# Attention backward, last units of the core: dK on two sets of 32x32 array tiles and dQ transposed in halves

## Chip, cores, metric

The kernel runs on one core of a Trainium2 chip. The metric is the device time of one execution in microseconds (us), smaller is better.

## What is computed

The reference concatenates two attention blocks over 2048 tokens of width 448 and returns the output and all gradients. The part that the change touches is the backward pass of block B (16 heads of width Dh = 28, one shared K and V head):

```python
def _B_ref(x, wq, wk, wv, wo):
    q = (x @ wq).reshape(B, S, H, Dh).transpose(0, 2, 1, 3)
    k, v = x @ wk, x @ wv
    p = softmax(einsum("bhqd,bkd->bhqk", q, k) * Dh ** -0.5)
    o = einsum("bhqk,bkd->bhqd", p, v)
    return o.transpose(0, 2, 1, 3).reshape(B, S, H * Dh) @ wo
_out, _vjp = jax.vjp(_f, ...)       # both blocks
_grads = _vjp(grad_out)
```

Out of it come dQ, dK and dV, and from these the gradients of the input (`out_4`, here dx), of wq (`out_5`), wk, wv (`out_6`, `out_7`) and wo (`out_8`).

## The kernel before

Block A and the projections of block B come first and fill some 215 us. The rest is one software pipeline, written out by hand under `manual_schedule` (in it every engine and queue keeps the order of the program): a loop over `u` from 0 to 539. A *unit* is 256 keys by two heads by 256 queries; a *block* `b` (of 64) is 8 units. Unit `u` computes scores for `u` (while `u < 512`), the product with dO for `w = u - 16`, its dS (VectorE L936 for one head; ScalarE L938 and GpSimd L939 for the other), the sums for o and dQ, the transposed dS for `y = u - 18`, and on odd `u` four of a block's 16 steps of dK (`dk_m`, L839). From `u = 512` on no scores are left: these last 28 units are the drain.

- **dK.** One step `dk_m` is four matmuls of 32 rows by 32 columns by 512 moving columns, on the diagonal tiles (32a, 32a) of the array; all add into one PSUM bank, `dk_acc`. In the drain the odd units 519 to 537 do it.
- **dQ** of block `b` is copied into `qT_B[g]` (L955), the last block at `u = 531`. At `u = 531` four DMA transposes of 128x2048 (L995, SyncE queue, one for each `g`) make `dqn`, dQ by tokens, which the gradient of wq needs.
- **Loads for the tail** (`post_load`, every even `u` from 512 to 528, SyncE queue): four loads of the output gradient (L757), four of x (L762), at `u = 528` the transposed weights `wqT` (L752). Behind that last one 14 small GpSimd DMAs (L754) put four rows each of the transposed wk and wv into unused rows of `wqT`. They overwrite what the load has brought, so they wait for it.
- **Gradient of wo** (`gwo`, from `u = 520`): 64 matmuls in PSUM banks SB[0] and SB[1]; each of four results is copied by ScalarE (L775) and stored by four GpSimd DMAs (L778, 16 in all). The last two output tiles of block B (`out_proj`, `u = 532` and 536) use SB[2] and are stored by GpSimd (L729).
- **The tail**, after the loop, is ordered by the scheduler, which may also pull its instructions up between those of the loop. VectorE copies dV out of PSUM (L1021, four), VectorE and ScalarE copy dK in turn (L1026, L1028, two each), both into `dkvT`. Then 14 small DMAs, the *pads* (L1067, seven on SyncE, seven on GpSimd in turn), put rows of `dkvT` into unused rows of `qT_B`, so that one product with `wqT` gives all of dx. TensorE does `dwq(0)`, `dwq(1)` (gradient of wq, from `dqn`) with the transposes of `dkvT`, `dx(0)` to `dx(4)`, `dwq(2)`, `dwq(3)`, the gradients of wk and wv, and `dx(5)` to `dx(15)`. The PSUM banks rotate: `dwq(2)` writes the bank of `dx(0)`.

```python
for n, (g, r, c) in enumerate(PADS):     # g = n // 4; c: row of dkvT, dK for n < 7, dV from n = 7 on
    [nc.sync, nc.gpsimd][n % 2].dma_start(qT_B[g].rearrange("(j r) s -> j r s", r=32)[:, r, :], dkvT[c:c + 4, :])
```

Of the kernel before, what the change touches and what calls it, by code (L numbers as in the profile page):

```python
# [8 lines left out]
ACT = mybir.ActivationFunctionType  # L9
ALU = mybir.AluOpType  # L10
AX = mybir.AxisListType
BF16 = mybir.dt.bfloat16
F32 = mybir.dt.float32

H = 16
DH = 28
D = 448
P = 128
# [7 lines left out]
def kernel(  # L26
# [21 lines left out]
    nc = tc.nc  # L48
# [3 lines left out]
    scale = float(DH) ** -0.5  # L52
# [35 lines left out]
    def flat(t):  # L88
        return t.rearrange("p a b -> p (a b)")
# [537 lines left out]
    NB = 64  # L627
    NU = NB * 8
    qT_B = [R1[:, g, :] for g in range(4)]
    vaug, kn, do_nat = vaug_, kn_, R2x[:, 0:NS, :]  # L630
    with ExitStack() as cs_:
        pe_ = cs_.enter_context(tc.tile_pool(name="ceT", bufs=1, side="right"))
        pn_ = cs_.enter_context(tc.tile_pool(name="ceN", bufs=1, side="right"))
        pd_ = cs_.enter_context(tc.tile_pool(name="cdsT", bufs=5, side="right"))
        pqa_ = cs_.enter_context(tc.tile_pool(name="cqXa", bufs=1, side="right"))
        px_ = cs_.enter_context(tc.tile_pool(name="cdsx", bufs=2, side="right"))
# [4 lines left out]
        SB = [psA.tile([P, 512], F32, name="aacc") for i in range(3)]  # L641
        DB = [psA.tile([P, 512], F32, name="agen") for i in range(2)]
        oq, dk_acc = (psA.tile([P, 512], F32, name="agen") for _ in range(2))

        dsT, dsx, qX, don, doT, rl, prod = ({} for _ in range(7))
        ETs = [pe_.tile([P, 4, 2, 512], BF16, name=f"eT{i}") for i in range(5)]
        ENs = [pn_.tile([P, 32, P], BF16, name=f"eN{i}") for i in range(6)]
# [7 lines left out]
        def mmt(out, lhsT, rhs, pos, start, stop):  # L655
            nc.tensor.matmul(out, lhsT=lhsT, rhs=rhs, start=start, stop=stop, tile_position=pos,  # L656
                             skip_group_check=True)

        def blk(b):
            qc, pair = divmod(b, 8)  # L660
            return qc, pair, pair // 2, pair % 2

        def rows_SD(u, sp, dp):
            b, tp = divmod(u, 8)
            w = u - 16
            qc, pair, g, hp = blk(b)
            todo = [(0, 0), (0, 1), (1, 0), (1, 1)] * 2
            if sp is not None and dp is not None and u % 2 == 0:
                todo = [(0, 0), (0, 1), (1, 0)] * 2 + [(1, 1)] * 2
            seen = {}  # L670
            for d in todo:
                if (dp if d[0] else sp) is None:
                    continue
                k, h = d
                t2 = seen.get(d, 0)
                seen[d] = 1
                t = 2 * tp + t2
                tc_ = slice(t * P, (t + 1) * P)
                oc = slice(t2 * 256, (t2 + 1) * 256)
                r = 64 * (1 - hp if k else hp) + 32 * h  # L680
                if k:
                    mmt(dp[h][:, oc], vT_rep[r:r + 32, tc_], doT[w // 8][r:r + 32, :], (r, 0), True, True)
                else:
                    mmt(sp[h][:, oc], kT_rep[r:r + 32, tc_], qT_B[g][r:r + 32, qc * 256:(qc + 1) * 256],
                        (r, 0), True, True)
# [45 lines left out]
        def by_tokens(t):  # L731
            return t.rearrange("p (t d) -> p t d", d=512)

        post = {"gb": [], "xb": []}
# [30 lines left out]
        def gwo(n0, n1):  # L765
            for n in range(n0, n1):
# [6 lines left out]
                if st == NS - 1:  # L773
                    sb = pd_.tile([P, 2, 512], BF16, name="dsT")[:, 0, 0:D]
                    nc.scalar.activation(out=sb, in_=al[:, 0:D], func=ACT.Copy)  # L775
                    for j in range(4):
                        h = 4 * g_ + j
                        nc.gpsimd.dma_start(out_8[h * DH:(h + 1) * DH, :], sb[32 * j + 1:32 * j + 1 + DH, :])  # L778

        GW = [0, 0, 4, 4, 10, 10, 16, 16, 22, 22, 28, 28, 34, 34, 40, 40, 48, 48, 56, 56, 64, 64]  # L780
        onps, tps2 = {}, {}

# [53 lines left out]
            nc.sync.dma_start_transpose(qX[qc].rearrange("p b s c -> p (b s) c")[:, :, g * P:(g + 1) * P],  # L836
                                        st.rearrange("p n a j -> p (n a j)"))

        def dk_m(b, m):  # L839
            qc, pair, g, hp = blk(b)  # L840
            h, B, s = m // 8, (m // 2) % 4, m % 2
            for a in range(4):
                rhs = dsx[b][32 * a:32 * a + 32, :, h, :, :].rearrange(
                    "p u t (b i s) -> p u t b i s", b=4, s=2)[:, :, :, B, :, s]
                mmt(dk_acc[32 * a:32 * a + 32, :],
                    qX[qc][32 * a:32 * a + 32, B, s, pair * 64 + 32 * h:pair * 64 + 32 * h + 32],
                    rhs, (32 * a, 32 * a), b == 0 and m == 0, b == NB - 1 and m == 15)

        def o_mm(v):
            b, tp = divmod(v, 8)  # L850
# [16 lines left out]
        def o_dq(vs, ys):  # L867
            for v, y in zip(vs, ys):
                todo = [f(i) for f, i in ((o_mm, v), (dq_mm, y)) if 0 <= i < NU]
                for _ in range(2):  # L870
                    for g_ in todo:
                        next(g_)

        def dv_mm(dv_acc, b, h, qb):
            for c in range(4):
                rhs = eN(b, c).rearrange("p (u h t q) k -> p u h t q k", u=2, h=2,
                                                       t=2)[:, :, h, :, qb, :]
                mmt(dv_acc[32 * c:32 * c + 32, :], don[b][:, qb, h, :], rhs, (0, 32 * c),
                    b == 0 and h + qb == 0, b == NB - 1 and h + qb == 2)
# [15 lines left out]
        with tc.manual_schedule():  # L895
            nc.sync.dma_start(wo, wo_d[:, 0:D].rearrange("(g p) c -> p g c", p=P))
            qX[0] = pqa_.tile([P, 4, 2, 512], BF16, name="qX")
            for g in range(4):
                st = pd_.tile([P, 2, 512], BF16, name="dsT").rearrange("p a (n j) -> p a n j", j=32).rearrange(
                    "p a (n b) j -> p (a n) b j", b=4)  # L900
# [3 lines left out]
            for u in range(NU + 28):  # L904
                w = u - 16
                hasS = u < NU
                hasD = 0 <= w < NU
                sp = [SB[(2 * u + h) % 3] for h in range(2)] if hasS else None
                dp = DB if hasD else None
                spare = SB[(2 * u + 2) % 3] if hasS else SB[2]  # L910
                rows_SD(u, sp, dp)
                if (b := due(u, 10)) is not None:
                    onat_T(b, spare)
# [11 lines left out]
                if u == 1:  # L925
                    q_shift(pn3, shifts[3], [pd_.tile([P, 2, 512], BF16, name="dsT").rearrange("p a b -> p (a b)").bitcast(F32)
                                             for _ in range(1)])
                    dv_acc = psA.tile([P, 512], F32, name="aacc")
# [24 lines left out]
                if (b := due(u, 27)) is not None:  # L953
                    qc, pair, g, hp = blk(b)
                    nc.vector.tensor_scalar(out=qT_B[g][64 * hp:64 * hp + 64, qc * 256:(qc + 1) * 256],  # L955
                                            in0=oq[64:128, 0:256], scalar1=scale, scalar2=None, op0=ALU.mult)
# [20 lines left out]
                if u % 2:  # L977
                    b, i = divmod(u - 27, 8)
                    if 0 <= b < NB:
                        for m in range(2 * i, 2 * i + 4):  # L980
                            dk_m(b, m)
                else:
                    o_dq((u - 2, u - 1), (u - 20, u - 19))
                    b, n = divmod(u - 20, 8)
                    for k in {0: (0, 1), 2: (2,), 6: (3,)}.get(n, ()) if 0 <= b < NB else ():
                        dv_mm(dv_acc, b, k // 2, k % 2)
                y = u - 18

                if 512 <= u < 530 and u % 2 == 0:
                    post_load((u - 512) // 2)  # L990
                if u == 531:
                    dqn = px_.tile([P, 8, 2, 2, 256], BF16, name="dsx").rearrange("p a b c d -> p (a b c d)").rearrange(
                        "p (t d) -> p t d", d=512)
                    for g_ in range(4):
                        nc.sync.dma_start_transpose(dqn[:, :, g_ * P:(g_ + 1) * P], qT_B[g_])  # L995
                if u >= 519:
                    gwo(GW[u - 519], GW[u - 518])

                if 0 <= y < NU:
                    b, tp = divmod(y, 8)  # L1000
                    if tp == 0:
                        dsx[b] = px_.tile([P, 8, 2, 2, 256], BF16, name="dsx")
                    nc.vector.transpose(  # L1003
                        out=dsx[b][:, tp, :, :, :].rearrange("p h t c -> p (h t c)").bitcast(F32),
                        in_=dsT[y][:, :, :].rearrange("p h c -> p (h c)").bitcast(F32))

        dkvT, wqT, xb = post["dkvT"], post["wqT"], post["xb"]
# [10 lines left out]
            return pd_.tile([P, 2, 512], BF16, name="dsT")[:, 0, :]  # L1018

        for c in range(4):  # L1020
            nc.vector.tensor_copy(out=dkvT[32:64, c * 512:(c + 1) * 512], in_=dv_acc[32 * c:32 * c + 32, :])  # L1021
        for c in range(4):
            t = dkvT[0:32, :].rearrange("p (t a i) -> p t a i", a=4, i=32)[:, :, c, :]
            src = dk_acc[32 * c:32 * c + 32, :].rearrange("p (t i) -> p t i", i=32)
            if c % 2:
                nc.vector.tensor_scalar(out=t, in0=src, scalar1=scale, scalar2=None, op0=ALU.mult)  # L1026
            else:
                nc.scalar.activation(out=t, in_=src, func=ACT.Copy, scale=scale)  # L1028

        def dwq(c):  # L1030
            r = DC_ROWS[c]
            al = gen(0)
            for st in range(NS):
                rhs = dqn[:, st, :].rearrange("p (h c) -> p h c", c=32)[:, :, 1:1 + DH]
                if c == 3:
                    half_mm(al, xb[st][:, 3 * P:D], rhs, st)
                else:
                    mm(al[:, 0:D], xb[st][:, c * P:(c + 1) * P], rhs, start=(st == 0), stop=(st == NS - 1))
            sb = sbuf()[:, 0:D]
            if c == 3:  # L1040
                odd = pd_.tile([P, 2, 512], BF16, name="dsT").rearrange("p a b -> p (a b)").bitcast(F32)[0:64, 0:D]
                nc.scalar.activation(out=odd, in_=al[64:128, 0:D], func=ACT.Copy)
                nc.vector.tensor_tensor(out=sb[0:64], in0=al[0:64, 0:D], in1=odd, op=ALU.add)
            else:
                nc.vector.tensor_copy(out=sb[0:r], in_=al[0:r, 0:D])
            nc.sync.dma_start(out_5[c * P:c * P + r, :], sb[0:r])
# [27 lines left out]
        for c in range(2, 4):  # L1074
            dwq(c)
        for c in range(4):
            r = DC_ROWS[c]
            ps = gen(0)
            for st in range(NS):
# [3 lines left out]
                                 func=ACT.Copy)  # L1083
# [35 lines left out]
```

## Time and profile before

| | |
|---|---|
| median of 3 runs | 1066.45 us (1065.12 to 1068.38) |
| span of the profiled execution | 1064.7 us |
| TensorE busy over the span | 1023.1 us (96%) |
| VectorE, ScalarE, GpSimd busy | 899.5 (84%), 870.4 (82%), 780.7 us (73%) |
| 16 DMA engines, hardware queue of SyncE | 99.6% of the span |
| dK steps of the drain begin | 1000.65 us (`u` = 519) ... 1030.11 us (`u` = 537) |
| `dwq(0)`, `dx(0)`, `dwq(2)` begin on TensorE | 1033.27, 1040.65, 1044.87 us |
| last matmul begins, span ends | 1060.39 (four of them), 1064.7 us |

Times inside the profile are us from the start of the span. The profiled execution's span of 1064.7 us is 1.75 us below the median of the timed runs. A line of the timeline gives start, length, engine, line of the kernel, operation, written and read tiles and count; behind it the idle time before it and what ended that. An entry of the GpSimd queue that is a DMA is the time in which GpSimd makes its descriptors; its data land later.

### The profile page before, as it was taken

The page shows a single profiled execution, that of the slowest core. Times are in us where ns is not written, and L with a number is a line of the kernel's source. Part 1 is how long each engine was busy: PE and PEld are TensorE (multiplying, and loading weights), DVE is VectorE, ACT ScalarE, POOL GpSimd, SP SyncE. Part 2 cuts the span into 40 slices and gives each one's busy share as a digit, 9 for nine tenths or more (in the row PEclk, how much of TensorE's full clock was granted, in tenths as well). Part 3 has the DMA queues.
Part 4 walks back from the last instruction along what each step waited for, and adds up shares of the span by engine and source line. Part 5 has one row for each costly group of instructions (what it writes and reads, how often), then busy time and mean ns, then how long its engine had stood idle before and what let it go on. Part 6 is the DMA issues. An engine that isn't in the chain of part 4 may idle for free.

```text
span 1064.7 us, 40036 instructions
## 1 busy us (share of the span) xinstructions
PE 1023.1 (96%) x16241; PEld 489.1 (46%) x16241; DVE 899.5 (84%) x1797; ACT 870.4 (82%) x1741; POOL 780.7 (73%) x1033
## 2 busy tenths in 40 slices
PE   9999999998999999999999999999999999999998
PEld 5555455434444444444444444444444444444444
DVE  7887400459999999999999999999999999999942
ACT  6463222489999999999999999999999999999522
POOL 6001242218888898899889989988998999888881
PEclk9999999999999999999999999999999999999999
DMA  9849899079999999999999999999999999999963
GB/s 264 167 108 192 171 203 246 22 137 181 193 188 196 182 203 189 188 202 191 197 181 197 181 196 195 193 189 194 196 197 192 199 190 183 208 190 177 222 141 89
DMA packets 689937, 195.15 MB, mean 183 GB/s; under 512 B 670616, under 2 KB 687792, under 8 KB 689752
## 3 DMA queue, kind: packets, MB, share of 16 engines
q1 hardware_dynamic: 680152, 179.92, 99.6%
q0 software_dynamic: 4640, 8.71, 2.9%
q10 hardware_dynamic: 4960, 3.96, 1.3%
q8 instruction: 127, 2.08, 0.8%
q14 instruction: 58, 0.48, 0.2%
HBM read 12.60 MB, written 10.84 MB: 22 GB/s over the span
## 4 chain that ended last, share of the span: by engine, by line
PE 43%; ACT 32%; issue 14%; POOL 5%; DVE 4%; DMA 1%; ACTq 0%; DVEq 0%; POOLq 0%
ACT cp L938 16%; PE agen L81 14%; ACT eT L970 13%; PE agen L656 10%; PE aacc L656 10%; PE aacc L81 5%; POOL dsT L939 3%; PE aacc L790 2%; ACT eT L924 2%; PE aacc L821 1%; DVE dsT L936 1%; DVE dsx L1003 1%; DMA out_dram<-dsT 1%; POOL eT L754 1%; POOL out_dram L778 0%
## 5 line engine op out<-in xcount | busy, mean ns | idle before, releaser
L939 POOL TENSOR_TENSOR dsT<-cp,eT 128x512 bf16<-128x512 bf16 x512 | 587.9, 1156 | 78.9 <-ACT cp L938 71.7
L1003 DVE STREAM_TRANSPOSE dsx<-dsT 128x512 f32<-128x512 f32 x512 | 357.6, 699 | 2.9 <-POOL dsT L939 0.8
L656 PEld LDWEIGHTS <-R 32*128 32x128 bf16 (+1 forms) x9104 | 227.9, 94 | 274.1 <-issue 238.4
L936 DVE TENSOR_TENSOR dsT<-agen,eT 128x512 bf16<-128x512 f32 x512 | 341.7, 667 | 10.9 <-PE agen L656 5.6
L938 ACT ACTIVATE cp<-agen 128x512 bf16<-128x512 f32 x512 | 315.8, 617 | 12.3 <-PE agen L656 11.2
L924 ACT ACTIVATE eT<-aacc 128x512 bf16<-128x512 f32 x512 | 313.6, 612 | 14.8 <-PE agen L656 4.8
L970 ACT ACTIVATE eT<-aacc 128x512 bf16<-128x512 f32 x512 | 322.2, 629 | 0.0
L656 PE MATMUL agen<-dsx,qX 32*32 32x512 bf16 x4096 | 267.6, 375 | 0.0
L656 PE MATMUL agen<-doT,R 32*128 32x256 bf16 x2048 | 247.1, 269 | 3.4 <-DVE dsT L936 1.4
L656 PE MATMUL aacc<-R,R 32*128 32x256 bf16 (+1 forms) x2240 | 218.2, 268 | 7.2 <-DVE oTs L800 2.5
L656 PE MATMUL agen<-eT,R 128*32 128x256 bf16 x2048 | 157.5, 274 | 0.1
L656 PE MATMUL agen<-dsT,R 128*32 128x256 bf16 x2048 | 156.8, 274 | 0.1
L656 PEld LDWEIGHTS <-qX 32*32 32x32 bf16 x4096 | 79.8, 89 | 113.7 <-issue 53.3
L656 PE MATMUL aacc<-eN,don 128*32 128x512 bf16 x1024 | 97.1, 379 | 0.1
L81 PEld LDWEIGHTS <-R 128*128 128x128 bf16 (+1 forms) x517 | 40.8, 98 | 43.5 <-issue 11.5
L406 POOL COPY pk<-R 128x256 bf16<-128x256 bf16 x4 | 1.6, 397 | 73.8 <-DVE R L366 73.7
L81 PE MATMUL agen<-R,R 128*128 128x448 bf16 (+1 forms) x180 | 42.1, 361 | 0.6 <-ACT R L225 0.6
L832 POOL COPY qst<-R 128x512 bf16<-128x512 bf16 x56 | 34.2, 611 | 4.0 <-DMA qX<-qst 3.9
L656 PEld LDWEIGHTS <-don 128*32 128x32 bf16 x1024 | 33.8, 97 | 1.4 <-issue 1.0
L804 POOL TENSOR_TENSOR prod<-R,oTs 128x128 f32<-128x128 bf16 x64 | 27.6, 431 | 9.3 <-DVE oTs L800 9.3
L422 DVE TENSOR_TENSOR osb<-aacc,pr 64x448 bf16<-64x448 f32 x2 | 1.2, 618 | 38.3 <-DMA out_dram<-osb 24.4
L955 DVE TENSOR_SCALAR R<-agen 64x256 bf16<-64x256 f32 x64 | 27.3, 427 | 3.6 <-PE agen L656 1.6
(231 smaller groups left out, 967.8 us busy)
## 6 DMA issues: line engine op xcount, KB each, us to landing
out_dram<-osb ACTq DMA_DIRECT2D x22, 112.0 KB
eN<-eT SPq DMA_TRANSPOSE x128
xa<-in_A_x_dram SPq DMA_DIRECT2D x8, 224.0 KB
ga<-in_grad_out_dram SPq DMA_DIRECT2D x4, 448.0 KB
xa<-in_grad_out_dram POOLq DMA_DIRECT2D x4, 448.0 KB, 6.1
out_dram<-wdq POOLq DMA_DIRECT2D x8, 224.0 KB, 4.0
eT<-in_grad_out_dram SPq DMA_DIRECT2D x4, 448.0 KB
eT<-in_B_x_dram SPq DMA_DIRECT2D x4, 448.0 KB
```

The lines of the kernel that those rows point to most:

```text
L81: nc.tensor.matmul(out_ap, lhsT=lhsT, rhs=rhs, start=start, stop=stop, tile_position=(0, 0))
L656: nc.tensor.matmul(out, lhsT=lhsT, rhs=rhs, start=start, stop=stop, tile_position=pos, skip_group_check=True)
L790: nc.tensor.transpose(onp[:, qb, :, :].rearrange("p h c -> p (h c)"), oTs[0:64, qb * P:(qb + 1) * P], identF[0:64, 0:64], tile_position=(0 ...
L804: nc.gpsimd.tensor_tensor(out=prod[b][:], in0=dnv, in1=os_, op=ALU.mult)
L832: eng.tensor_copy(out=st.rearrange("p (b s) a j -> p b s a j", s=2)[:, :, s, :, :], in_=src.unsqueeze(2).to_broadcast([P, 4, 4, 32]))
L924: nc.scalar.activation(out=eT(u)[:, 0, :], in_=sp[0][:, :], func=ACT.Exp, scale=scale)
L936: nc.vector.tensor_tensor(out=dst[:, 0, :], in0=dp[0][:, :], in1=ew[:, 0, :], op=ALU.mult)
L938: nc.scalar.activation(out=cp[:, :], in_=dp[1][:, :], func=ACT.Copy)
L939: nc.gpsimd.tensor_tensor(out=dst[:, 1, :], in0=cp[:, :], in1=ew[:, 1, :], op=ALU.mult)
L955: nc.vector.tensor_scalar(out=qT_B[g][64 * hp:64 * hp + 64, qc * 256:(qc + 1) * 256], in0=oq[64:128, 0:256], scalar1=scale, scalar2=None, ...
L970: nc.scalar.activation(out=eT(u)[:, 1, :], in_=sp[1][:, :], func=ACT.Exp, scale=scale)
L1003: nc.vector.transpose(out=dsx[b][:, tp, :, :, :].rearrange("p h t c -> p (h t c)").bitcast(F32), in_=dsT[y][:, :, :].rearrange("p h c -> p ...
```

## The change

Four edits, all in the drain and the first lines of the tail. In the odd units 519 to 535 every second dK step uses the tiles (32a, 32((a+2) mod 4)) and adds into a bank of its own, `dk_two` = SB[2]; unit 537 goes on as before. The last two output tiles move from SB[2] to DB[1] and DB[0]. dQ by tokens is no longer made at `u = 531` by four transposes of 128x2048, but by eight of 128x1024 into two freed buffers of transposed e: two at `u = 523`, two at 525, two at 527, one at 529, one at 531. dV is copied by ScalarE at `u = 533`, `dk_two` (scaled, with the rows put back) by ScalarE at `u = 536`, and VectorE adds the two halves of dK in four instructions in place of the four copies.

```diff
+        dqn = [by_tokens(flat(ENs[(124 + c) % 6])) for c in range(2)]
...
-        def dk_m(b, m):
+        dk_two = SB[2]
+
+        def dk_m(b, m, other=0):
...
-                mmt(dk_acc[32 * a:32 * a + 32, :],
+                k = 32 * ((a + 2) % 4) if other else 32 * a
+                mmt((dk_two if other else dk_acc)[k:k + 32, :],
                     qX[qc][32 * a:32 * a + 32, B, s, pair * 64 + 32 * h:pair * 64 + 32 * h + 32],
-                    rhs, (32 * a, 32 * a), b == 0 and m == 0, b == NB - 1 and m == 15)
+                    rhs, (32 * a, k), other == 2 or b == 0 and m == 0, other == 0 and b == NB - 1 and m == 15)
...
-                spare = SB[(2 * u + 2) % 3] if hasS else SB[2]
+                spare = SB[(2 * u + 2) % 3] if hasS else DB[u // 4 % 2] if u > 530 else SB[2]
...
-                            dk_m(b, m)
+                            dk_m(b, m, (1 + (u == 519 and m == 2 * i + 1)) * (m % 2) if 519 <= u < 537 else 0)
...
                 if 512 <= u < 530 and u % 2 == 0:
                     post_load((u - 512) // 2)
-                if u == 531:
-                    dqn = px_.tile([P, 8, 2, 2, 256], BF16, name="dsx").rearrange("p a b c d -> p (a b c d)").rearrange(
-                        "p (t d) -> p t d", d=512)
-                    for g_ in range(4):
-                        nc.sync.dma_start_transpose(dqn[:, :, g_ * P:(g_ + 1) * P], qT_B[g_])
+                for v, half, gs in ((523, 0, (0, 1)), (525, 0, (2, 3)), (527, 1, (0, 1)), (529, 1, (2,)), (531, 1, (3,))):
+                    for g_ in gs if u == v else ():
+                        nc.sync.dma_start_transpose(dqn[half][:, :, g_ * P:(g_ + 1) * P],
+                                                    qT_B[g_][:, half * 1024:half * 1024 + 1024])
+                if u == 533:
+                    for c in range(4):
+                        nc.scalar.activation(out=post["dkvT"][32:64, c * 512:(c + 1) * 512], in_=dv_acc[32 * c:32 * c + 32, :],
+                                             func=ACT.Copy)
+                if u == 536:
+                    dk_sum = pd_.tile([P, 2, 512], BF16, name="dsT").rearrange("p a b -> p (a b)").bitcast(F32)
+                    for c in range(2):
+                        r = 64 * (1 - c)
+                        nc.scalar.activation(out=dk_sum[64 * c:64 * c + 64, :], in_=dk_two[r:r + 64, :], func=ACT.Copy,
+                                             scale=scale)
...
-            nc.vector.tensor_copy(out=dkvT[32:64, c * 512:(c + 1) * 512], in_=dv_acc[32 * c:32 * c + 32, :])
-        for c in range(4):
...
-            if c % 2:
-                nc.vector.tensor_scalar(out=t, in0=src, scalar1=scale, scalar2=None, op0=ALU.mult)
-            else:
-                nc.scalar.activation(out=t, in_=src, func=ACT.Copy, scale=scale)
+            nc.vector.scalar_tensor_tensor(out=t, in0=src, scalar=scale,
+                                           in1=dk_sum[32 * c:32 * c + 32, :].rearrange("p (t i) -> p t i", i=32),
+                                           op0=ALU.mult, op1=ALU.add)
...
-                rhs = dqn[:, st, :].rearrange("p (h c) -> p h c", c=32)[:, :, 1:1 + DH]
+                rhs = dqn[st // 8][:, st % 8, :].rearrange("p (h c) -> p h c", c=32)[:, :, 1:1 + DH]
```

## Prediction

> **What bounds it now.** I read four views: TensorE's timeline of the drain, GpSimd's, SyncE's, and last the chain of waits. TensorE has no idle time from 1000.33 to 1020.28 and then only two gaps, 0.44 us before the second half of the gradient of wo and 0.50 us before `dwq(0)` (its 128x2048 transposes land late). So shorter dK steps do move TensorE forward. But GpSimd's timeline shows a second engine that never rests:
>
> ```profile
> 1012.10 2.45 POOL L939 TENSOR_TENSOR dsT<-cp,eT 128x512 bf16<-128x512 bf16 x2 [1.39 <-DVE dsT L936]
> 1015.72 1.16 POOL L939 TENSOR_TENSOR dsT<-cp,eT 128x512 bf16<-128x512 bf16 x1 [1.17 <-ACT cp L938]
> 1017.19 7.98 POOL L754 DMA_DIRECT2D eT<-wkvT_d  x14 [0.32 <-issue]
> 1025.17 4.06 POOL L778 DMA_DIRECT2D out_dram<-dsT  x8
> 1030.11 0.57 POOL L729 DMA_DIRECT2D out_dram<-R  x1 [0.88 <-DMA out_dram<-dsT]
> ...
> 1033.30 1.70 POOL L1067 DMA_DIRECT2D R<-eN  x3
> 1035.00 2.07 POOL L778 DMA_DIRECT2D out_dram<-dsT  x4
> 1037.06 2.25 POOL L1067 DMA_DIRECT2D R<-eN  x4
> ```
>
> 39 small DMAs run back to back from 1017.19 to 1039.31: 7.98 (14 x L754) + 8.13 (16 x L778) + 1.12 (2 x L729) + 3.95 (7 pads, L1067) = 21.2 us, plus 0.88 us of waiting. The last pads are dK rows that `dx` needs; a pad lands 2.1 us after its start, the last one at 1040.8. `dx(0)` begins at 1040.65, so TensorE and GpSimd arrive together today. What starts GpSimd's row is in the chain of waits, which goes through it:
>
> ```profile
> 1012.10 1.16 POOL dsT L939
> 1013.28 3.21 DMA eT<-wqT_d
> 1017.19 1.27 POOL eT L754 x3
> ...
> 1038.23 1.08 POOL R L1067 x2
> 1039.31 11.86 issue
> ```
>
> The 14 DMAs wait for the landing of `wqT` (1013.28 + 3.21 = 1016.49) and stand behind GpSimd's last product (1016.88). SyncE's queue, which issues that load:
>
> ```profile
> 996.61 1.25 SPq L961 DMA_TRANSPOSE R<-R  x1
> 997.96 2.13 SPq L757 DMA_DIRECT2D eT<-in_grad_out_dram  x3
> 1000.20 9.61 SPq L762 DMA_DIRECT2D eT<-in_B_x_dram  x4
> 1013.28 0.37 SPq L752 DMA_DIRECT2D eT<-wqT_d  x1
> 1018.70 12.25 SPq L995 DMA_TRANSPOSE dsx<-R  x4
> ```
>
> `wqT` has idle DMA engines today, and the transposes come after it. The windows show how full they were before it (next to last column: DMA share, last: GB/s):
>
> ```profile
> 1000.00:1009.70 9.70, 9.67 (x123) 3.92 (x120) 8.22 (x15) 5.37 (x11) 7.17 (x8) 1.00 1.11 297
> 1009.70:1010.50 0.80, 0.80 (x7) 0.43 (x6) 0.80 (x2) 0.78 (x2) 0.80 (x1) 1.00 0.15 45
> 1010.50:1012.50 2.00, 2.00 (x27) 0.57 (x25) 1.26 (x3) 0.66 (x2) 0.61 (x2) 1.00 0.85 232
> ```
>
> The loads of units 512 to 524 saturate the engines until 1009.7; only the load of unit 526 and `wqT` are left.
>
> **dK, a gain on TensorE.** Sixteen matmuls of a unit take 1.04 us, one 0.385: four sets begin (1.04 - 0.385)/3 = 0.218 us apart, the four tiles of a set together. With eight tiles two sets run at once: 2 x 0.218 = 0.44 us saved, in nine units 3.9 us. That eight can run has neighbours in the trace: at 802.84 eight matmuls of 128x32 on four column tiles (four streams out of the same rows) take 0.60 us, and at 800.54 four row tiles start within 0.01 us into different banks. Bounds: 0 if two streams with stride do not go together, 3.9 if they do; I take 3.9, nearest to these rows.
>
> **Copies.** ScalarE is idle from 1016.3 to 1020.1 and from 1021.1 to 1026.9; four copies of dV at about 0.6 us (L1028: 0.59) and two of `dk_two` hide there. If they did not, dV would come later by 2.4 us, still ahead of dK. The four sums on VectorE: below, four at 0.59 (the shortest of today's four), above at 0.69 (L1026); I take 0.69, 2.8 us against 2.65 today (1031.20 to 1033.85). The last dK step ends at 1031.1 - 3.9 = 1027.2, so `dkvT` is whole at 1030.0, ahead of its transposes on TensorE at about 1033; what is left of this path is the pads. SB[2] to DB: DB is free after unit 527, nothing.
>
> **Transposes, gain and cost.** The gap of 0.50 us goes. `dwq(0)` begins at 1033.27 - 0.50 - 3.9 = 1028.9; TensorE reaches `dx(0)` 7.38 us later (today 1033.27 to 1040.65), at 1036.3. Next late are the pads, through GpSimd. Six half transposes now stand in SyncE's queue ahead of `wqT` (units 523, 525, 527; its load is in 528). The wait they add is for the dV product of unit 522, done at about 1005; behind them stand the loads of units 524, 526 and 528. SyncE could still issue `wqT` near 1013.5 (six at 1.25 to 1.3 us and three loads at 0.4 from 1005 on), but the data queue up: the transposes begin with the backlog that today ends at 1009.7. Price of one: below 0.87 us (262 KB at 302 GB/s, the rate of the loads between 1001 and 1009), above 2.02 (longest of the 28 of the same size, L836; median 1.30). Nearest are those 1.30 and half of today's own, 12.25/8 = 1.53; I take 1.4, six are 8.4 us. So `wqT` lands at 1009.7 + 1.53 (load of unit 526, 459 KB at 302) + 8.4 + 1.5 (itself) + 0.3 = 1021.4 in place of 1016.5. The other waiters on this queue lose nothing: the load of unit 526 lands by about 1017 and the last two transposes by about 1024.5 (1021.4 + 2.8), both ahead of `dwq(0)` at 1028.9.
>
> The Trainium skill, "DMA: Bandwidth & Descriptors", section "Latency and other measured facts", gives a DMA transpose 261 GB/s; the estimate by this page is 1.0 us for a half, 2.4 us less for six, and a time near 1069. The transposes of this trace are slower (2.1 MB in 12.25 us is 171 GB/s).
>
> **GpSimd then.** Its row begins at 1021.4, not 1017.19; the 0.88 goes, since no transposes disturb its later stores (by unit 531 they are issued; if it stays, 0.9 more). The last but one pad, the second that `dx(0)` needs first, lands at 1021.4 + 21.2 - 0.55 + 1.5 = 1043.5. TensorE stands from 1036.3 to 1043.5. Against 1040.65 this is +2.9 us; less 0.28 of a wait for a copy that `dx(1)` has today, plus 0.2 for the next pad: +2.8. No other work fills the gap, since `dwq(2)` writes the bank of `dx(0)`; all behind it is TensorE work and moves along.
>
> **Clock.** The trace shows a price for such a stop. The granted clock is 1.00 until 1063.4 and 0.50 from 1063.5 on, 2.2 us after the last matmul; and the first matmuls of the span (nine of 128x512 from 1.29 on) begin 0.427 us apart, half speed, for 4.0 us. Cost of 7 us idle: below 0, above 4 us at half speed, 2.0 lost; I take 2.0, since the stop is over three times 2.2.
>
> The Trainium skill, "TensorE: Matmul & The Clock Gate", section "Part 1: The HAM clock gate", puts one window at 3.4 us, idle to throttle, busy to release; the estimate by it is 1.7 in place of 2.0, and a stop under 3.4 us might cost nothing. It speaks against a change that makes TensorE wait this long.
>
> **Sum.** Profiled execution 1064.7 + 2.8 + 2.0 = 1069.5; the median lies 1.75 higher: 1071.3 us.
>
> **Rivals.**
> - *GpSimd is not delayed* (the other side). If `wqT` lands no later than today, the row follows GpSimd's last product, 4 x 0.44 = 1.75 us earlier: 1015.4. `dx(0)` at 1037.5, TensorE idle 1.3 us, no clock loss: -3.2, 1063.3 us. If the dK pads also come ahead of the last four stores, TensorE alone decides: -3.9 - 0.5 - 0.28, 1061.8. For it: SyncE issues in time. Against: the full engines before 1009.7. Even at no cost of clock the row must start before 1018.6 to win, with it before about 1016.6. Chance 0.15.
> - *Delay, but cheap*: transposes near 0.87 us give `wqT` at 1018.2, -0.4 + 2.0 = +1.6, 1068.1; or the scheduler puts the dK pads ahead of the last four stores (2.07 us earlier), +2.7, 1069.2. Chance 0.30. Against: those stores stand before the last pads today.
> - *Eight tiles do not run at once*: the change doesn't do what it says. TensorE comes at 1040.15 in place of 1036.3, waits 3.4 us: the same end, 1071.3, as GpSimd sets it. In the chances it is part of the forecast.
>
> **Numbers.** Forecast 0.55, cheap delay 0.30, no delay 0.15. 0.3% (3.2 us) is about what a measurement of this kernel tells from no change. Slower by more: 0.45 of the forecast's 0.55, where the row starts after about 1019.8. Same: its other 0.10, the cheap delay, 0.02 of no delay: 0.42. Faster: 0.13. At 2.02 a transpose `wqT` lands at 1025.1, 1075.0. Range: 1063.5 to 1074.5 leaves out most of the gain and the highest price.
>
> **What would show it.** Right: dK units of 0.6 us; `dwq(0)` near 1028.9 with no wait; L754 starting after 1020; a gap of several us before `dx(0)`, ended by a pad; matmuls behind it twice as far apart. Wrong: L754 at 1017 or earlier, or pads ahead of the L778 stores.

## The result and the profile after

The changed kernel takes 1074.27 us (median of 6 runs, 1069.93 to 1075.52) against 1066.62 us (1065.12 to 1068.61) for the kernel before on the same chip: ratio 1.0061, 95% interval [1.0047, 1.0075]. It is slower. The forecast was 1071.3, 4.9 us more than before; measured is 7.7 us more by the medians and 6.5 by the ratio. 1074.27 lies inside the range, but only 0.2 us below its upper end.

The profiled execution has a span of 1073.8 us, 9.0 more. 2.64 us of this lie ahead of unit 519, where the change edits nothing. Most of them have a cause of their own: in block A the granted clock of this execution is 0.50 for 3.41 us from 51.05 on, which costs some 1.7 us, and in the profile of before it is 1.00 there. The profiles of e8, e9 and e10 have this drop too; in these four unit 519 begins at 1002.1 to 1003.3 us, in the eight without it at 999.4 to 1000.7. So stages are compared from the first dK matmul of unit 519 on:

| us behind unit 519 | `wqT` issued | L754 row starts | `dwq(0)` | `dx(0)` | `dwq(2)` | span ends |
|---|---|---|---|---|---|---|
| before | 12.63 | 16.54 | 32.62 | 40.00 | 44.22 | 64.07 |
| after | 17.47 | 22.76 | 29.74 | 44.22 | 49.78 | 70.47 |

TensorE reaches `dwq(0)` 2.9 us earlier and `dx(0)` 4.2 us later; from there to `dwq(2)` it needs 1.3 us more, and 0.8 more to the end. The same views as before show how. SyncE's timeline (start, length, queue, line, operation, tiles, count):

```profile
1005.79 6.36 SPq L997 DMA_TRANSPOSE eN<-R  x2
1012.25 0.52 SPq L762 DMA_DIRECT2D eT<-in_B_x_dram  x1
1012.83 3.90 SPq L997 DMA_TRANSPOSE eN<-R  x2
1016.84 0.52 SPq L762 DMA_DIRECT2D eT<-in_B_x_dram  x1
1017.40 3.24 SPq L997 DMA_TRANSPOSE eN<-R  x2
1020.75 0.52 SPq L752 DMA_DIRECT2D eT<-wqT_d  x1
```

Three pairs of transposes stand ahead of the load of `wqT`, and the issue of a pair takes 3.2 to 6.4 us, so that SyncE comes to this load 4.84 us later than before (17.47 for 12.63 in the table). The chain of waits carries this on:

```profile
1018.74 1.91 SPq L997
1020.75 4.76 DMA eT<-wqT_d
1026.04 1.27 POOL eT L754 x3
...
1046.02 1.10 POOL R L1077 x2
1047.12 12.20 issue
1059.33 4.11 DMA out_dram<-dsT
```

`wqT` lands 4.76 us after its issue (3.21 before), and GpSimd's row hangs on it. GpSimd's timeline, with the idle time before an entry and what ended it in brackets:

```profile
1018.10 1.17 POOL L943 TENSOR_TENSOR dsT<-cp,eT 128x512 bf16<-128x512 bf16 x1 [1.18 <-ACT cp L942]
1026.04 7.87 POOL L754 DMA_DIRECT2D eT<-wkvT_d  x14 [6.78 <-DMA eT<-wqT_d]
...
1044.86 2.26 POOL L1077 DMA_DIRECT2D R<-eN  x4
```

GpSimd has nothing to do for 6.78 us, then issues the same 39 DMAs without a pause until 1047.12. TensorE's timeline shows who waits for the last of them:

```profile
1007.24 0.39 PE L656 MATMUL agen<-doT,R 32*128 32x256 bf16 x4 [0.21 <-DVE dsT L940]
...
1019.60 0.41 PE L656 MATMUL agen<-dsx,qX 32*32 32x512 bf16 x4
1019.62 0.41 PE L656 MATMUL aacc<-dsx,qX 32*32 32x512 bf16 x4
...
1047.51 0.53 PE L81 MATMUL aacc<-eT,R 128*128 128x448 bf16 x1 [6.94 <-DMA R<-eN]
...
1064.65 0.92 PE L81 MATMUL agen<-eT,R 128*128 128x448 bf16 x4 [1.09 <-DVE dsT L1071]
```

The two dK lines show eight tiles at work: four into one bank (`agen`), four into the other (`aacc`), begun 0.02 us apart. Then TensorE stands 6.94 us for a pad. A window behind `dx(0)` (busy time and count of PE, PEld, DVE, ACT, POOL, then granted clock, DMA share, GB/s) gives the price of the stop:

```profile
1048.40:1051.00 2.60, 2.60 (x9) 1.06 (x7) 0.00 (x0) 0.00 (x0) 0.00 (x0) 0.50 0.00 0
```

At a clock of 0.50 nine matmuls are at work in these 2.60 us, begun 0.37 us apart; from 1051.30 to 1053.10 the clock is 1.00 again, and they begin 0.19 us apart.

### The profile page after: what moved, and what is told of

It reads as the page before. It is cut to its first block, busy times and chain, and to the rows that moved or that the text cites. A ratio compares the mean times of both kernels' runs of the same rounds, so it can differ in the third digit from the quotient of the medians.

```text
span 1073.8 us, 40038 instructions
## 1 busy us (share of the span) xinstructions
PE 1022.0 (95%) x16232; PEld 489.6 (46%) x16241; DVE 897.5 (84%) x1795; ACT 873.0 (81%) x1745; POOL 781.7 (73%) x1033
## 4 chain that ended last, share of the span: by engine, by line
PE 42%; ACT 31%; issue 14%; POOL 7%; DVE 5%; DMA 1%; SPq 0%; ACTq 0%; DVEq 0%; POOLq 0%
ACT cp L942 16%; PE agen L81 14%; ACT eT L974 13%; PE aacc L656 10%; PE agen L656 9%; PE aacc L81 5%; POOL dsT L943 4%; PE aacc L791 2%; ACT eT L928 2%; DVE dsT L940 1%; DVE dsx L1016 1%; PE aacc L822 1%; POOL out_dram L778 1%; POOL eT L754 1%; DMA eT<-wqT_d 0%
## 5 line engine op out<-in xcount | busy, mean ns | idle before, releaser
L940 DVE TENSOR_TENSOR dsT<-agen,eT 128x512 bf16<-128x512 f32 x512 | 342.0, 668 | 10.4 <-PE agen L656 5.1
L656 PE MATMUL agen<-dsx,qX 32*32 32x512 bf16 x4024 | 264.4, 376 | 0.2 <-issue 0.2
L81 PE MATMUL aacc<-eT,R 128*128 128x448 bf16 x96 | 23.2, 366 | 7.4 <-DMA R<-eN 6.9
```

The lines of the kernel that those rows point to most:

```text
L81: nc.tensor.matmul(out_ap, lhsT=lhsT, rhs=rhs, start=start, stop=stop, tile_position=(0, 0))
L940: nc.vector.tensor_tensor(out=dst[:, 0, :], in0=dp[0][:, :], in1=ew[:, 0, :], op=ALU.mult)
```

## The experiments

Theory 1 is the prediction's: the six half transposes ahead of `wqT` delay GpSimd's row, and that alone makes the kernel slower. The rivals, by their numbers in the expectations: the new copies and sums come late (2); the data of the transposes crowd the DMA engines whatever their place in a queue (3); the pads land late for another reason than GpSimd's issuing (4). All ratios are to the kernel before, timed on the same chip.

### e1: the change with the transposes as before

```diff
-                for v, half, gs in ((523, 0, (0, 1)), (525, 0, (2, 3)), ...):
-                    ...
+                if u == 531:
+                    dqn = px_.tile([P, 8, 2, 2, 256], BF16, name="dsx")...
+                    for g_ in range(4):
+                        nc.sync.dma_start_transpose(dqn[:, :, g_ * P:(g_ + 1) * P], qT_B[g_])
```

> The change without its new transposes: dK on eight tiles, the copies of dV and of the second bank on ScalarE and the four sums on VectorE stay; dQ by tokens is made as before, by four transposes of 128x2048 at unit 531. Theory 1 (the transposes ahead of wqT in SyncE's queue delay it, GpSimd's row of small DMAs behind it starts late, the pads land late): wqT lands 3 to 4 us after its issue again, GpSimd's row starts within 1 us of the end of its last product, TensorE waits 0 to 2.5 us at dx(0), and the kernel is 1 to 3 us faster than before, 1063.5 to 1065.5. Rival 2 (the pads are late since the new sums of dK and the copies on ScalarE come late): the wait of 7 us at dx(0) stays, 1072 to 1075.

Measured: 1068.01 us, ratio 1.0004 [0.9992, 1.0016]. The size failed. `wqT` is issued at 12.51 and GpSimd's row starts at 16.45 us behind unit 519, as early as expected, and `dx(0)` waits for no pad; so the delay of 6.2 us is the transposes' work and rival 2 falls. But TensorE now arrives at `dwq(0)` before the late transposes have landed (e1, TensorE):

```profile
1032.13 5.64 PE L81 MATMUL aacc<-dsx,eT 128*128 128x448 bf16 x20 [2.57 <-DMA dsx<-R]
```

The 2.57 us also halved the clock for 3.4 us: the 20 matmuls take 5.64 us, 4.21 in e7. Shorter dK steps without earlier transposes turn into a wait. Not every run pays for the clock: in four of the twelve its mean is 1.000.

### e2: the kernel before with the transposes of the change

```diff
+        dqn = [by_tokens(flat(ENs[(124 + c) % 6])) for c in range(2)]
-                if u == 531: ...
+                for v, half, gs in ((523, 0, (0, 1)), (525, 0, (2, 3)), (527, 1, (0, 1)), (529, 1, (2,)), (531, 1, (3,))):
+                    ...
```

> The kernel before with the new transposes alone (eight of 128x1024 from unit 523 on); dK on four tiles and the copies as before. Theory 1: wqT lands some 8 us later than before, GpSimd's row too, TensorE comes 3 us later to dx(0) than in the changed kernel and so waits some 4 us less than its 7 but starts dx(0) at the same place behind the drain: 1071 to 1074. Rival 2 (sums and copies): no wait at dx(0), 1065 to 1067.

Measured: 1073.42 us, ratio 1.0055 [1.0040, 1.0069]. The row starts at 22.70, 6.2 us later than before (some 8 were expected), `dx(0)` at 44.52 after an idle 4.90 us, the end is at 71.03: the change's own end within 0.6 us, with none of its dK edits. TensorE in e2:

```profile
1044.21 0.53 PE L81 MATMUL aacc<-eT,R 128*128 128x448 bf16 x1 [4.90 <-DMA R<-eN]
```

The transposes alone carry the loss, and the time that dK saves only lengthens the wait (4.90 to 6.94 us).

### e3: the change, six half transposes behind the load of `wqT`

```diff
-((523, 0, (0, 1)), (525, 0, (2, 3)), (527, 1, (0, 1)), (529, 1, (2,)), (531, 1, (3,)))
+((528, 0, (0, 1, 2, 3)), (528, 1, (0, 1)), (529, 1, (2,)), (531, 1, (3,)))
```

> The whole change, but its first six half transposes are issued at unit 528 behind the load of wqT, the others at 529 and 531 as in the change. Theory 1: wqT lands 3 to 4 us after its issue, GpSimd's row starts 1 to 2 us earlier than before, the dK pads land at about 22 us behind that, TensorE waits 1 to 2 us at dx(0) with no loss of clock: 2 to 3.5 us faster than before, 1063 to 1064.5. If the transposes cost by their own work wherever they stand (rival 3: the engines are full in the drain), dwq(0) or the pads wait for them and it is slower than before by 2 us or more.

Measured: 1065.68 us, ratio 0.9982 [0.9970, 0.9994]. The order of one queue is the difference between the ratios 1.0061 and 0.9982, and the loss of 2 us or more that rival 3 asks for didn't come. The gain on before, 1.9 us by the ratio, is just under the 2 to 3.5 expected: GpSimd's row starts 16.86 us behind unit 519, 0.3 later than before and not 1 to 2 earlier, and the pads still end a wait before `dx(0)` (e3, TensorE):

```profile
1039.05 0.35 PE L81 MATMUL aacc<-eT,R 128*128 128x448 bf16 x1 [1.46 <-DMA R<-eN]
```

Its matmuls follow 0.19 us apart: 1.46 us of idling cost no clock.

### e4: the change, `wqT` loaded through ScalarE's queue

```diff
-                nc.sync.dma_start(post["wqT"], ...)
+                nc.scalar.dma_start(post["wqT"], ...)
```

> The whole change with the transposes where it puts them, but the load of wqT is issued by ScalarE's queue in place of SyncE's. Theory 1 in its narrow form (what delays wqT is its place behind the transposes in one queue): wqT lands within 4 us of an issue at about 10 us behind unit 519, the wait at dx(0) is under 2.5 us, 1063 to 1066. Rival 3 (the 16 DMA engines are full, so it is late from any queue): it takes 6 us or more to land, the wait at dx(0) is 3 us or more, 1068 to 1072.

Measured: 1069.98 us, ratio 1.0023 [1.0010, 1.0035], between the two. The issue comes at 14.32, 3.15 us earlier than in the change and 1.7 later than before. GpSimd's timeline of e4:

```profile
1019.30 7.84 POOL L754 DMA_DIRECT2D eT<-wkvT_d  x14 [3.96 <-DMA eT<-wqT_d]
```

GpSimd waits until 19.94, 5.6 us after the issue (3.9 before), and TensorE for a pad:

```profile
1039.49 0.53 PE L81 MATMUL aacc<-eT,R 128*128 128x448 bf16 x1 [2.83 <-DMA R<-eN]
```

So the place in SyncE's queue is a bit under half of the delay: the other queue alone regains 2.8 us of 6.2. Of the 3.4 left, 1.7 are the later issue on ScalarE (it was expected at 10 us; why it came at 14.32 is open) and 1.7 the longer way from issue to row, with the transposes under way at the same time. This last part is what rival 3 says. e3 regains all but 0.3 us, as there the transposes' data come behind the load as well.

### e5: the change, GpSimd's pads on ScalarE's queue

```diff
-            [nc.sync, nc.gpsimd][n % 2].dma_start(qT_B[g]...
+            [nc.sync, nc.scalar][n % 2].dma_start(qT_B[g]...
```

> The whole change, transposes ahead of wqT as it puts them, but the seven pads of GpSimd's queue are issued by ScalarE's queue. Theory 1 (the late wqT hurts only through GpSimd's row of 39 small DMAs, at whose end the pads stand): wqT and the start of the row are as late as in the changed kernel (row at about 22.7 us behind unit 519), but TensorE waits under 1 us at dx(0), which begins 37 to 38.5 us behind unit 519 in place of 44.2, no loss of clock: 1064 to 1066, at least 6 us under the changed kernel. Rival 4 (dx waits for wqT and the rows that are put into it, not for the pads): the wait stays above 3 us, 1069 or more.

Measured: 1065.41 us, ratio 0.9980 [0.9970, 0.9990]. GpSimd's row is as late as in the change (it starts at 23.10), but no pad stands in it; the waits of TensorE in e5 have none for a pad, and `dx(0)` begins at 37.16:

```profile
PE agen L656 <- DVE dsT L940: 1.0, 4, 0.4
PE agen L81 <- DVE dsT L1071: 0.8, 1, 0.8
PE aacc L81 <- ACT dsT L775: 0.4, 1, 0.4
PE aacc L81 <- DVE dsT L1053: 0.2, 1, 0.2
```

Rival 4 falls: what makes `dx(0)` late is that the pads are issued behind GpSimd's other DMAs.

### e6: the change, TensorE kept busy before `dx(0)`

```diff
+        for _ in range(36):
+            mm(oq[:, 0:D], xb[0][:, 0:P], dqn[0][:, 0, 0:D])
         for st in range(5):
             dx(st)
```

> The whole change, and 36 matmuls of 128x448 into an idle PSUM bank ahead of dx(0), whose results nobody reads: they fill the 7 us in which TensorE waits. Clock theory: the granted clock stays at 1.00, dx(0) begins at the same place behind unit 519 (44.2 us), dwq(2) 3.8 to 4.2 us behind dx(0) in place of 5.6; 1.5 to 2 us under the changed kernel, 1072 to 1073. If the slower dx came from something else (pads landing one by one, copies), nothing changes: 1074 to 1075.

Measured: 1072.25 us, ratio 1.0040 [1.0028, 1.0052]. In e6's timeline of TensorE the added matmuls fill the gap (33 of the 36 are in the trace):

```profile
1037.51 6.41 PE L81 MATMUL agen<-eN,eT 128*128 128x448 bf16 x33
1044.95 0.35 PE L81 MATMUL aacc<-eT,R 128*128 128x448 bf16 x1 [1.03 <-DMA R<-eN]
```

The clock stays at 1.00, and `dx(0)` to `dwq(2)` takes 4.27 us in place of 5.56: the clock's share of the loss is 1.3 us on this stretch. (e6's profile also lacks the last wait for VectorE, so its whole gain on the change, ratio 1.0040 for 1.0061 or some 2.2 us, isn't the clock's alone.)

### e7 and e8: `wqT` first and pads off GpSimd

e7 is e3 and e5 together. e8 also moves the last stores:

```diff
-            nc.gpsimd.dma_start(out_7[...
+            nc.scalar.dma_start(out_7[...
```

> The change with both cures: the first six half transposes behind the load of wqT (as in the run with wqT first) and the seven pads of GpSimd on ScalarE's queue. Theory 1: no wait at dx(0), which begins at 37.3 to 37.7 us behind unit 519 (before: 40.0); what the change gains on TensorE arrives: 2 to 3 us faster than before, 1064 to 1065. Under rival 4 it is no better than the run with wqT first.

> The run with both cures, and the four stores of the gradient of wv (out_7) issued by ScalarE's queue in place of GpSimd's. If the wait of 1.1 to 1.3 us ahead of the fifth of the last dx is for the landing of these GpSimd stores (dx takes over their buffers), it falls to 0.3 us or less: 1 us under the run with both cures, 3 to 4 us faster than before, 1063 to 1064. If it is for other stores, no difference.

Measured: e7 1064.49 us, ratio 0.9973 [0.9964, 0.9983]; e8 1065.36 us, ratio 0.9974 [0.9963, 0.9985]. Both beat the kernel before, and by what can be told, equally. A part of their gain is the drop of the clock in block A: the mean clock shows it in 10 of the 24 runs of before, in none of the 8 of e7 and in one of the 9 of e8. Among the runs without it e7 and e8 are both 2.5 us faster by the mean. In e7's waits of TensorE one has grown (1.1 us in the change):

```profile
PE agen L81 <- DVE dsT L1071: 1.7, 1, 1.7
```

VectorE's copies of `dx` wait for buffers there, as it seems: the chain of the change has 4.11 us of landing of GpSimd's stores of `out_7` in this place. In e8 these go through ScalarE and the wait is gone from the profile (span end 61.25 behind unit 519, 62.83 in e7). The times don't show those 1.6 us, so whether it gains is open.

### e9 and e10: is it dK or the pads that gains?

e9 is the kernel before with e5's edit alone; e10 is e7 without all dK edits (tiles, banks, sums and the copies of dV).

> The kernel before with one edit: the seven pads of GpSimd go to ScalarE's queue. Theory (the gain of the two versions that beat the kernel before comes from the shorter dK steps; moving the pads only lets it through): the kernel before had no wait at dx(0), TensorE and GpSimd arrived together, so nothing is won: dx(0) stays at 39.7 to 40.0 us behind unit 519 and the ratio is 0.999 to 1.001. Rival (the pads alone make the gain): the ratio is 0.996 to 0.998 and dx(0) begins before 39 us behind unit 519.

> The kernel before with half transposes, six of them behind the wqT load, and the pads on ScalarE's queue: the best version without the eight-tile dK steps. Theory (dK makes the gain): only the 0.5 us gap before dwq(0) and the 0.28 us behind dx(0) can go; dwq(0) begins at 31.9 to 32.3 us behind unit 519 (30.1 with the dK steps), dx(0) at 39.3 to 39.7 (37.5 with them), the ratio is 0.999 to 1.0005. Rival (order of the queues and pads make the gain, the dK steps nothing): ratio 0.9965 to 0.998, as with the dK steps.

Measured: e9 1071.02 us, ratio 1.0038 [1.0023, 1.0052], which neither theory had. e10 1067.36 us, ratio 0.9997 [0.9986, 1.0009], as the theory had it: `dwq(0)` at 31.96, `dx(0)` at 39.45 (30.13 and 37.50 in e7). So the dK edits, worth nothing in e1, are worth what separates e7 from e10 once neither transposes nor pads wait: 0.24% by the ratios, but 1.7 us among the runs without the clock's drop in block A (e7 2.5 us faster than before, e10 0.8), and 1.95 us at `dx(0)` in the profiles.

e9's loss is a new wait in ScalarE's queue. The pads overwrite rows of `qT_B` that the transposes read. ScalarE's timeline in e9:

```profile
1028.64 4.49 ACTq L1067 DMA_DIRECT2D R<-eN  x2
1033.24 0.54 ACT L775 ACTIVATE dsT<-aacc 128x448 bf16<-128x448 f32 x1 [10.66 <-PE agen L656]
```

dV was copied by 1023.96, but ScalarE stood in the wait of a pad from 1021.79 to 1028.60, and the second pad was issued at 1032.58, as the last of the four 128x2048 transposes (1028.21 to 1032.65) ended. The copy L775 behind it came late, and TensorE waited for that:

```profile
1037.74 4.89 PE L81 MATMUL aacc<-dsx,eT 128*128 128x448 bf16 x16 [1.85 <-ACT dsT L775]
```

The clock halved for 3.4 us here too. That the transposes are what the pads waited for is read from these times; it wasn't tried apart. In e5 and e7 the transposes begin earlier, and with the same edit TensorE waits neither for a pad nor longer for L775.

## Why the prediction was right

- **`wqT` behind the transposes.** The mechanism, a late `wqT` through transposes ahead of it, is shown by e2 and e3, its way over GpSimd's row by e5. The size was low: the load was forecast to land 4.9 us later and landed 6.4 us later, and GpSimd's row was forecast 4.2 us later and began 6.2 us later. The place was in part wrong too: the prediction let SyncE issue the load near 1013.5, about as today, and put the delay into queued data. In the profile the issue itself comes 4.84 us later, and only 1.55 us are the longer landing (4.76 for 3.21). Whether full engines held up SyncE's issue of the transposes, no run tells. Worked back with the forecast's own other terms, a half transpose cost 1.64 us, not 1.4 (`wqT` landed at 1025.51, 22.22 us behind unit 519, where six at 1.4 gave 20.75). The row chosen, transposes of another place in the kernel (1.30), was too cheap; half of today's own in the drain (1.53) was nearer.
- **GpSimd's row.** 21.2 us forecast, 21.07 measured (22.76 to 43.83); the 0.88 us went, as forecast. The rule that `dx(0)` follows the last but one pad was off by one pad: `dx(0)` began at 1047.51, when the last but two of GpSimd's pads had landed (1047.42) and the last but one had not (1047.99), and e2, e3 and e6 have the same 0.09 us behind the last but two. (In the profile before that pad landed at 1039.70, so GpSimd then had some 0.9 us to spare at `dx(0)`.) This put the forecast some 0.6 us too late and hid a part of the first error; that the idle time was 6.94 us against 7.2 is so in part luck.
- **dK.** This is the term that was furthest off: 3.9 us forecast, 2.4 measured (`dwq(0)` is 2.88 us earlier, 0.50 of it the gap). Eight tiles do run at once, and from a unit's dK to the next work it takes 0.57 to 0.59 us instead of 0.98 where no wait follows, which is 0.4 in each of nine units. But the pairs of sets follow 0.24 us apart, not 0.218, and TensorE now overtakes VectorE: four waits for dS (L940), 1.0 us together, that were hidden before. The prediction said of other stalls what is late next, not of this one. It cost the forecast nothing, as another engine set the end.
- **Gap before `dwq(0)`.** Gone, as forecast. (The last two transposes were to land by 1021.4 + 2.8, which is 1024.2 and not 1024.5; it changes nothing.) e1 shows that it would have become 2.57 us without the change's earlier transposes: the two parts of the change need each other.
- **Clock.** 2.0 us forecast; half speed for the 3.65 us from `dx(0)` to 1051.16, some 1.8 lost; e6 confirms the cause. (Only 1.3 us more than before show from `dx(0)` to `dwq(2)`, as the kernel before had waits of its own there, 0.28 us for a copy among them.)
- **Not forecast:** 0.8 us of waits near the end, for VectorE's copies of `dx` behind GpSimd's stores.
- **Sum.** Behind unit 519 the profile has 4.2 us at `dx(0)` (2.9 forecast), 1.3 from there to `dwq(2)` (1.9: the clock less 0.08 of other waits) and 0.8 at the end (none): 6.4 for 4.8. The ratio gives 6.5 us (5.0 to 8.0), so the 2.64 us that this one profile has ahead of unit 519 need no cause in the change. The direction and the waits are no luck, since e2 and e3 turn them on and off; that the range held, by 0.2 us, is.
- **Rivals.** "Not delayed" and "delay, but cheap" fall with the row's start at 22.76 and with the four pads that still stand last in it. "Eight tiles do not run at once" falls with the timeline; its remark that the end would be the same is what e2 shows.

## What to carry to other kernels

When work is put earlier in a DMA queue, name every transfer that it passes and follow each to its last waiter: here a 14-DMA row on an engine with under 1 us to spare. Shortening the busiest engine pays only to the point where the next resource is late, so find that one first; the dK edits were worth nothing in e1 and some 2 us in e7 against e10. Moving a waiting DMA to another engine's queue (e9) makes all that engine's later work wait with it.

## What the runs showed of the hardware

The granted clock moves on a grid. All stretches at one clock between two changes are whole multiples of 3.413 us (in the change 44.373, 3.413, 989.865 and 6.827). The drop came at the end of a grid step that held about 2 us or more of time without a matmul: 2.3 us of it in e1 (a stop of 2.57), 2.0 in e4 (2.83), 2.2 in e9 (0.47 and 1.85). It didn't come for a stop of 1.46 us in e3 or 1.71 us in e7, which the grid cuts in two. Over the twelve profiles every full-clock step with 1.94 us or more of it was followed by half clock (21 steps, the ends of the spans among them), and none with 1.83 us or less. The half clock then held for one step where the next had 0.3 us or less of idle time (e1, e9) and for two where it had 0.8 us or more (e4, e2, the change), so two stops of like length cost 3.4 or 6.8 us at half speed. The drop in block A fits too: its step has 1.94 us in the four profiles that drop there, and at most 1.4 us in the others, whose grid lies otherwise.

The Trainium skill, "TensorE: Matmul & The Clock Gate", section "Part 1: The HAM clock gate", has the same free-running window of 3413 ns, but counts on an idle window of that length for a throttle; these runs show that 57% of one (1.94 us) is enough and 54% (1.83 us) is not.
